# Token mixing of the second batch by one joint product, and its last two attention pairs as whole pairs

## Chip, cores, metric

The program runs on one core of one Trainium2 chip. The metric is device time in microseconds (us) of one execution, and the median over runs is compared. Engines are named as the profile names them: PE is TensorE (PEld its weight loads), DVE is VectorE, ACT is ScalarE, POOL is GpSimd, SP issues the DMAs.

## What is computed

Three stages follow each other for 4 batches of 768 tokens. Gated linear attention has 8 heads of 48 channels, so 384 channels together; a token and channel MLP follows, and a gating unit behind it.

```python
state = alpha[:, :, t, :, None] * state + np.einsum('bhd,bhe->bhde', k[:, :, t], v[:, :, t])
y[:, :, t] = np.einsum('bhd,bhde->bhe', q[:, :, t], state)
...
h = xt @ U @ V
u = x + h.transpose(0, 2, 1)
ch = np.maximum(u @ w_ch1, 0.0) @ w_ch2
return (u + ch).astype(np.float32)
```

The product with U (768 x 32) over the tokens, and with V (32 x 768) back to them, is the token mixing; the two products with w_ch1 and w_ch2 are the channel MLP. The gating unit is not touched by the change.

## The kernel before

Data lie with channels on the 128 partitions, in KE = 3 blocks of channels (m = 0, 1, 2) and NB = 2 blocks of 384 tokens. Products that need float32 accuracy are made of two fp32r parts, a high part and the remainder, in three matmuls (mm3, L287 to L289, and up_group, L380), or as plain float32 matmuls, which the trace shows as more than one pass of PE.

**Order of the work.** Every engine runs its instructions in the order in which the Python code issues them. The first batch's attention runs alone (first_batch). Then the channel MLP of batch b is issued group by group, and between its matmuls pull() is called, which advances a generator by a step: attend(b + 1), the attention and token mixing of the next batch. For b = 0 the pulls also move the loading and splitting of the MLP's weights, by the table FIRST_STEPS (L75): "f" is finish, one piece of a late step (ACT's high part L785, then DVE's remainder L252), "b" begins the next weight (DVE L237, L240, L247), "s" is a step of the attention. due() spaces the steps: with b = 0 some 40 steps go into 65 pulls, with later b 42 into 129, so the attention of the second batch is issued about twice as densely as that of the third and fourth.

**One attention pair.** attend handles a batch as NP = 4 pairs of heads, n = b * NP + i, in the order (3, 0, 1, 2) of their channel blocks. Eight steps make a pair: flip (L958 transposes k, ACT copies it, L961); prepare for the next pair (DVE's scan L914, reciprocal L917, and a multiplication L903 of k, on DVE or POOL); added (L1002, sums of k and v per chunk) and state, in which ACT writes the decay into a PSUM bank (L1009) and copies the sums (L1010), and DVE runs six scans (L1013); keep, two ACT copies of the state (L1023, L1024); scores (L974) and mask (DVE); the second part of prepare (scan L927, L903 of q); outputs; loading of a later pair.

A Pair has outputs in two parts: inner (L1034, masked scores and v) and outer (L1044, state and q). A WholePair has the scores of one head beside the q of the other in one operand, and v beside the state in the other, so one product per chunk (L1103) makes both. For that its place() copies half of q by a DMA (sq, L1080) and loads v into the free half of the state's tile (two DMAs, L1083), and its mask takes four operations (L1091) in place of two (L984). In the kernel before, the pairs of the third and fourth batch are WholePairs, since place() is called for n + 1 >= 2 * NP.

**Token mixing.** In the second batch, class Mix takes each channel block by itself, one pair later: flip (L1213, three transpositions per token block), a copy by ACT (L1220), product (L1229, six float32 matmuls of 128 columns with U) and keep (L1236, DVE L1237). In later batches JointMix collects all three blocks: ACT copies the high part of a flipped block (L1258), DVE makes the remainder in two operations (L1260), and one product over 384 columns (L1266 and L1279, fp32r) and keep (L1282, L1284) follow behind the last pair. split_u makes U's parts for that (ACT L1289 and three of L1292, DVE L1293). mix_sum (L318) then multiplies with V, DVE adds (L322), ACT makes the high part (L323) and POOL the remainder (L252). At the batch's end the MLP's results are added by L440; L387 and L368 are its high part and remainder of h.

**Banks.** PSUM banks 5 and 6 are the pair's (PAIR), 7 is ALONE. Flips use ALONE and the first of PAIR; the second mixing flip and the product of Mix use ALONE, and so does the decay:

```python
decay = ps.banks[:, ALONE, TB : TB + DS * NCH]
...
mix.take(mix.flip(1, ALONE))
pair.state(pair.added())
```

Of the kernel before, what the change touches and what calls it, by code (L numbers as in the profile page):

```python
# [46 lines left out]
E = H * D  # L47
# [29 lines left out]
    60: "b", 70: "ff", 80: "b", 89: "ff", 92: "b", 101: "fbf", 110: "ff",  # L77
# [23 lines left out]
def gla_mixer_gating_kernel(ctx: ExitStack, tc: tile.TileContext, akq, v, v2, vT, u, v3, w12, w_in, wsT, b_sp, w_out, out):  # L101
# [699 lines left out]
    with ExitStack() as fast:  # L801
# [95 lines left out]
        def scale(x, by, n):  # L897

            cut = NCH if n == 0 or by is bw and NP <= n < 2 * NP - 1 else 0
            half = NCH // 2 if n == 0 and by is fw else 0  # L900
            for engine, c in ((nc.vector, slice(0, half)), (nc.vector, slice(half, cut)), (nc.gpsimd, slice(cut, NCH))):
                if c.stop > c.start:
                    engine.tensor_tensor(out=chunks(x)[:, c], in0=chunks(x)[:, c], in1=chunks(by)[:, c, 1:CW], op=ALU.mult)  # L903
# [398 lines left out]
        def attend(b, blocks):  # L1302
# [3 lines left out]
            joint = b > 1  # L1306
            stk = up.pool.tile([(3 + joint) * R, E], F32R, name="stk", tag="stk")
            moves, mix = [], None
            if joint:
                if "u4" not in g:  # L1310
                    split_u()
                whole = JointMix(us, stk)
# [8 lines left out]
            for i in range(NP):  # L1321
# [5 lines left out]
                pair.flip()  # L1327
                if mix:
# [20 lines left out]
                if mix and not joint:  # L1349
                    gp = mix.product(0, ALONE)  # L1350
                pair.outputs()
                if mix and not joint:
                    mix.keep(gp)
                yield
                if n + 1 < NPAIR and n + 1 >= 2 * NP:
# [6 lines left out]
                mix = (whole if joint else Mix(us, pair.hp, stk)) if pair.hp < KE else None  # L1362
                if joint:
                    whole.m = pair.hp
                yield
            mix.take(mix.flip(0))
            mix.take(mix.flip(1))
            yield
            if joint:
                yield  # L1370
            gp = mix.product()
            if joint:
                yield
            mix.keep(gp)
            yield
            yield from mix_sum_steps(g, us, stk, up, ps, "x", blocks, whole.parts if joint else None)

        N_STEPS = NP * 8 + 2 + 2 * KE
# [31 lines left out]
        def first_batch(blocks):  # L1410
# [93 lines left out]
            weights.add()  # L1504
            summed(0, 0)
            summed(1, 0)
            gp = mixes[2].product()
            mixes[2].keep(gp)
            for blk in range(NB):
                summed(blk, 1)  # L1510
                summed(blk, 2)
# [87 lines left out]
        for b in range(B):  # L1599
            if b == 0:  # L1600
                n_steps = N_STEPS + N_AHEAD
            elif b + 1 < B:
                nxt = []
                steps, n_steps = attend(b + 1, nxt), N_STEPS + (2 if b > 0 else 0)
# [7 lines left out]
            groups = int(NB * NF1 * 2 * KE * (0.95 if b == 0 else 0.9))  # L1612
# [195 lines left out]
```

## Time and profile before

| what | us |
|---|---|
| median of 3 runs | 675.04 (674.24 to 675.76) |
| the profiled execution's own time | 675.9 |
| its span in the profile | 674.2 |
| PE busy (matmul) | 659.4, 98% of the span |
| DVE busy | 421.3, 62% |
| ACT busy | 306.4, 45% |
| POOL busy | 147.3, 22% |

The span runs from the first to the last instruction of the profiled execution; 1.7 us of its time lie around it. PE's share is so high that its few gaps are of interest, and what stands in them: the engine that releases it. The shares of the other engines are means over stages. While the first batch's MLP and the second batch's attention run together, from about 46 to 154 us, DVE also splits the MLP's weights and is much busier than its mean.

### The profile page before, as it was taken

To read this page: it belongs to the slowest core of one execution; us is meant where nothing else is said; L and a number is where in the kernel's file an instruction comes from. 1 tells how busy PE (TensorE), PEld (TensorE's weight loads), DVE (VectorE), ACT (ScalarE), POOL (GpSimd) and SP (SyncE) were. 2 spreads that over 40 slices of the span, in tenths; PEclk is the share of its full clock that TensorE was granted. 3 is DMA by queue.
4 is the path that set the end of the run, shared out by engine and by line. 5 is a ranking of instruction groups with operands and counts; after the bars stand their busy time and mean duration, and the time that the engine had idled before them with its cause. 6 is when DMAs were issued, how large, how long until landed. Compare 5 with 4: busy or idle time off the path is not lost.

```text
span 674.2 us, 13930 instructions
## 1 busy us (share of the span) xinstructions
PE 659.4 (98%) x5732; PEld 628.3 (93%) x5732; DVE 421.3 (62%) x808; ACT 306.4 (45%) x599; POOL 147.3 (22%) x139
## 2 busy tenths in 40 slices
PE   8989999899999999999999999999999999999996
PEld 7889999799999999999999999999999989999996
DVE  7989999668556435565236787486384356537541
ACT  3985467555555335555323445343343233334321
POOL 4530112133112132210120000306401620540051
PEclk9999999899999999999999999999999999999999
DMA  8799016433555501512112455401010202101011
GB/s 328 261 358 237 22 35 113 88 72 102 118 102 119 119 1 42 115 29 67 36 65 79 124 167 164 129 1 36 35 57 15 71 0 71 36 35 36 1 36 41
DMA packets 23561, 60.06 MB, mean 89 GB/s; under 512 B 3137, under 2 KB 13249, under 8 KB 22209
## 3 DMA queue, kind: packets, MB, share of 16 engines
q1 hardware_dynamic: 23488, 59.08, 32.0%
q8 instruction: 47, 0.77, 0.5%
q14 instruction: 26, 0.20, 0.1%
HBM read 46.88 MB, written 9.44 MB: 84 GB/s over the span
## 4 chain that ended last, share of the span: by engine, by line
PE 83%; DVE 12%; ACT 2%; issue 1%; DMA 0%; DVEq 0%; ACTq 0%
PE banks L380 19%; PE banks L287 18%; PE banks L289 18%; PE banks L288 18%; DVE bw L914 2%; PE banks L1103 2%; DVE fw L927 2%; DVE narrow L240 1%; PE banks L1002 1%; PE banks L974 1%; DVE w L252 1%; DVE narrow L247 1%; PE banks L958 1%; DVE hl L368 1%; PE banks L1229 1%
## 5 line engine op out<-in xcount | busy, mean ns | idle before, releaser
L380 PE MATMUL banks<-partuh,w 128*128 128x384 f32 x564 | 130.5, 339 | 1.9 <-DVE hl L368 1.8
L380 PEld LDWEIGHTS banks<-partuh,w 128*128 128x128 f32 x564 | 99.3, 188 | 3.6 <-DVE hl L368 2.4
L287 PE MATMUL banks<-h,w 128*128 128x384 f32 x288 | 98.1, 340 | 0.2
L289 PE MATMUL banks<-hl,w 128*128 128x384 f32 x288 | 96.4, 335 | 0.0
L288 PE MATMUL banks<-h,w 128*128 128x384 f32 x288 | 96.4, 335 | 0.0
L368 DVE SCALAR_TENSOR_TENSOR hl<-banks,h 128x384 fp32r<-128x384 f32 x96 | 52.7, 550 | 58.0 <-ACT h L387 56.9
L387 ACT ACTIVATE h<-banks 128x384 fp32r<-128x384 f32 x94 | 45.8, 487 | 78.6 <-PE banks L380 78.4
L252 POOL TENSOR_TENSOR partul<-ub,partuh 128x384 fp32r<-128x384 f32 x43 | 43.0, 1024 | 137.1 <-ACT partuh L457 83.7
L252 POOL TENSOR_TENSOR room<-room 128x384 fp32r<-128x384 f32 x32 | 32.6, 1018 | 164.4 <-ACT room L600 164.2
L380 PE MATMUL banks<-partul,w 128*128 128x384 f32 x282 | 66.0, 341 | 0.0
L903 POOL TENSOR_TENSOR akq<-akq,fw 128x768 f32<-128x768 f32 x14 | 23.7, 1693 | 148.2 <-DVE fw L927 96.8
L287 PEld LDWEIGHTS banks<-h,w 128*128 128x128 f32 x288 | 54.1, 188 | 1.6 <-issue 0.8
L288 PEld LDWEIGHTS banks<-h,w 128*128 128x128 f32 x288 | 54.1, 188 | 0.0
L289 PEld LDWEIGHTS banks<-hl,w 128*128 128x128 f32 x288 | 54.1, 188 | 0.0
L380 PEld LDWEIGHTS banks<-partul,w 128*128 128x128 f32 x282 | 49.2, 188 | 0.8
L600 ACT ACTIVATE room<-room 128x384 fp32r<-128x384 f32 x32 | 16.8, 526 | 67.5 <-DVE room L598 67.5
L252 DVE TENSOR_TENSOR vl<-vt,vh 128x512 fp32r<-128x512 f32 (+1 forms) x48 | 26.6, 616 | 20.7 <-ACT vh L505 20.7
L288 PE MATMUL banks<-partuh,winl 128*128 128x384 f32 x96 | 32.4, 338 | 0.0
L289 PE MATMUL banks<-partul,winh 128*128 128x384 f32 x96 | 32.4, 338 | 0.0
L287 PE MATMUL banks<-partuh,winh 128*128 128x384 f32 x96 | 32.4, 338 | 0.0
L288 PE MATMUL banks<-wouth,room 128*128 128x384 f32 x96 | 32.3, 336 | 0.0
L289 PE MATMUL banks<-woutl,room 128*128 128x384 f32 x96 | 32.3, 336 | 0.0
(256 smaller groups left out, 1479.2 us busy)
## 6 DMA issues: line engine op xcount, KB each, us to landing
akq<-in_akq SPq DMA_DIRECT2D x24, 434.4 KB, 7.7
bits<-in_w SPq DMA_DIRECT2D x12, 768.0 KB, 11.5
x2d<-ub SPq DMA_DIRECT2D x8, 576.0 KB, 3.7
ub<-x2d SPq DMA_DIRECT2D x8, 576.0 KB, 4.2
out_y<-room SPq DMA_DIRECT2D x24, 192.0 KB, 1.9
v<-in_v SPq DMA_DIRECT2D x15, 288.0 KB, 8.1
words<-in_wsT SPq DMA_DIRECT2D x7, 576.0 KB, 3.7
words<-in_w_in SPq DMA_DIRECT2D x8, 384.0 KB, 3.2
```

The lines of the kernel that those rows point to most:

```text
L252: engine.tensor_tensor(out=out, in0=x, in1=hi.bitcast(F32), op=ALU.subtract)
L287: nc.tensor.matmul(out=ps, lhsT=wh, rhs=xh, start=first, stop=False, skip_group_check=more)
L288: nc.tensor.matmul(out=ps, lhsT=wl, rhs=xh, start=False, stop=False, skip_group_check=more)
L289: nc.tensor.matmul(out=ps, lhsT=wh, rhs=xl, start=False, stop=last, skip_group_check=more)
L368: nc.vector.scalar_tensor_tensor(out=hl, in0=ps[:, 0:TB], scalar=0.0, in1=h.bitcast(F32), op0=ALU.max, op1=ALU.subtract)
L380: nc.tensor.matmul(out=ps[:, 0:TB], lhsT=wx[:, k * 128 : (k + 1) * 128], rhs=ux[:, k, :], start=i == 0, stop=i == len(parts) - 1)
L387: nc.scalar.activation(out=h, in_=ps[:, 0:TB], func=AF.Relu)
L600: nc.scalar.activation(out=hi, in_=x, func=AF.Copy)
L903: engine.tensor_tensor(out=chunks(x)[:, c], in0=chunks(x)[:, c], in1=chunks(by)[:, c, 1:CW], op=ALU.mult)
L914: nc.vector.tensor_tensor_scan(out=bw[:, ::-1], data0=a[:, 1 : AW + 1][:, ::-1], data1=ends[:, ::-1], initial=0.0, op0=ALU.mult, op1=ALU.max)
L927: nc.vector.tensor_tensor_scan(out=fw, data0=a[:, 0:AW], data1=starts, initial=0.0, op0=ALU.mult, op1=ALU.max)
L1103: nc.tensor.matmul(out=self.py[HW * h : HW * h + D, x, j * CH : (j + 1) * CH], lhsT=vw[:, h, c, :], rhs=self.sms[h][:, t], start=True, sto ...
```

## The change

1. The second batch (b = 1) uses JointMix for all three channel blocks. Its first two blocks are flipped in the fourth pair's steps (block 0 in place of the earlier flips, block 1's first half ahead of the fourth pair's outputs, the rest behind it), and one joint product follows. split_u runs at the fourth pair's flip.
2. The second batch's third and fourth pairs are WholePairs (n + 1 >= NP + 2), so their place() adds three DMAs each.
3. The third pair's q is multiplied by DVE in place of POOL (L903).
4. FIRST_STEPS: of "fbf" at pull 101 the last "f" goes to pull 107. The steps of the second batch rise by two, the pulls that they are spread over from 136 to 139.
5. In the first batch, all three products come ahead of the six sums, and these go in another order; the add of a weight (POOL) goes behind the third product.

```diff
-    60: "b", 70: "ff", 80: "b", 89: "ff", 92: "b", 101: "fbf", 110: "ff",
+    60: "b", 70: "ff", 80: "b", 89: "ff", 92: "b", 101: "fb", 107: "f", 110: "ff",
...
-            cut = NCH if n == 0 or by is bw and NP <= n < 2 * NP - 1 else 0
+            cut = NCH if n == 0 or by is bw and NP <= n < 2 * NP - 1 or by is fw and n == NP + 2 else 0
...
-            joint = b > 1
-            stk = up.pool.tile([(3 + joint) * R, E], F32R, name="stk", tag="stk")
+            late = b == 1
+            stk = up.pool.tile([4 * R, E], F32R, name="stk", tag="stk")
             moves, mix = [], None
-            if joint:
-                if "u4" not in g:
-                    split_u()
-                whole = JointMix(us, stk)
+            whole = JointMix(us, stk)
...
                 pair.flip()
+                if late and i == NP - 1:
+                    split_u()
                 if mix:
                     mix.take(mix.flip(0, PAIR[1]))
...
-                if mix and not joint:
-                    gp = mix.product(0, ALONE)
+                if late and mix:
+                    whole.m += 1
+                    mix.take(mix.flip(0, ALONE))
                 pair.outputs()
-                if mix and not joint:
-                    mix.keep(gp)
                 yield
-                if n + 1 < NPAIR and n + 1 >= 2 * NP:
+                if n + 1 < NPAIR and n + 1 >= NP + 2:
                     placed[n + 1] = WholePair(n + 1, None, None, tags)
...
-                mix = (whole if joint else Mix(us, pair.hp, stk)) if pair.hp < KE else None
-                if joint:
-                    whole.m = pair.hp
+                if late:
+                    mix, whole.m = whole if i == NP - 2 else None, 0
+                else:
+                    mix, whole.m = whole if pair.hp < KE else None, pair.hp
                 yield
+            if late:
+                mix, whole.m = whole, KE - 2
+                mix.take(mix.flip(1))
+                whole.m = KE - 1
             mix.take(mix.flip(0))
             mix.take(mix.flip(1))
...
-            weights.add()
-            summed(0, 0)
-            summed(1, 0)
             gp = mixes[2].product()
             mixes[2].keep(gp)
-            for blk in range(NB):
-                summed(blk, 1)
-                summed(blk, 2)
+            weights.add()
+            for blk, m in ((0, 0), (0, 1), (1, 0), (0, 2), (1, 1), (1, 2)):
+                summed(blk, m)
...
-            groups = int(NB * NF1 * 2 * KE * (0.95 if b == 0 else 0.9))
+            groups = int(NB * NF1 * 2 * KE * (0.97 if b == 0 else 0.9))
```

The order on DVE ahead of the second batch's third pair's scans, before (w is an MLP weight, narrow its raw form, sm the masked scores):

```order
L927 SCALAR_TENSOR_TENSOR fw<-akq_89,starts 128x780
L368 SCALAR_TENSOR_TENSOR hl<-banks,h 128x384
L914 SCALAR_TENSOR_TENSOR bw<-akq_87,ends 128x780
L917 RECIPROCAL starts<-bw 128x12
L368 SCALAR_TENSOR_TENSOR hl<-banks,h 128x384
L440 TENSOR_TENSOR ub<-banks,ub 128x384 x3
L237 TENSOR_SCALAR narrow<-bits 128x768
L240 SCALAR_TENSOR_TENSOR narrow<-bits,narrow 128x768
L247 ISA narrow<-bits,narrow 128x1536
L252 TENSOR_TENSOR w_1455<-narrow,w_1455 128x768
L1013 SCALAR_TENSOR_TENSOR after<-add,banks 128x96 x6
L984 TENSOR_TENSOR sm<-banks,causal 128x384 x2
```

and in the changed kernel, from the multiplication that comes in behind that first scan (sq is the copied half of q):

```order
L903 TENSOR_TENSOR akq_89<-akq_89,fw 128x768
L368 SCALAR_TENSOR_TENSOR hl<-banks,h 128x384
L914 SCALAR_TENSOR_TENSOR bw<-akq_87,ends 128x780
L917 RECIPROCAL starts<-bw 128x12
L368 SCALAR_TENSOR_TENSOR hl<-banks,h 128x384
L440 TENSOR_TENSOR ub<-banks,ub 128x384 x3
L237 TENSOR_SCALAR narrow<-bits 128x768
L240 SCALAR_TENSOR_TENSOR narrow<-bits,narrow 128x768
L247 ISA narrow<-bits,narrow 128x1536
L1013 SCALAR_TENSOR_TENSOR after<-add,banks 128x96 x6
L1091 TENSOR_TENSOR akq_89<-banks,causal 64x6x64 x2
L1091 TENSOR_TENSOR sq<-banks,causal 64x6x64 x2
```

The multiplication L903 of q is new, the remainder L252 ahead of the scans is gone, and four masks of L1091 stand where two of L984 did.

The order on DVE at the fourth pair, before (stk is the product with U):

```order
L927 SCALAR_TENSOR_TENSOR fw<-akq_87,starts 128x780
L1237 TENSOR_TENSOR stk<-banks,stk 32x128
L252 TENSOR_TENSOR w_1632<-narrow,w_1632 128x768
L368 SCALAR_TENSOR_TENSOR hl<-banks,h 128x384
L440 TENSOR_TENSOR ub<-banks,ub 128x384 x3
L914 SCALAR_TENSOR_TENSOR bw<-akq_88,ends 128x780
L917 RECIPROCAL starts<-bw 128x12
L1013 SCALAR_TENSOR_TENSOR after<-add,banks 128x96 x6
L984 TENSOR_TENSOR sm<-banks,causal 128x384 x2
```

and in the changed kernel (u is the split U, ynl and yl are remainders of a flipped block, of token block 0 with partuh and of block 1 with partul):

```order
L252 TENSOR_TENSOR w_1603<-narrow,w_1603 128x768
L1293 TENSOR_TENSOR u_1617<-uf,u_1617 128x6x32
L1260 TENSOR_TENSOR ynl<-banks,partuh 128x2x128
L1260 TENSOR_TENSOR yl<-banks,partuh 128x128
L368 SCALAR_TENSOR_TENSOR hl<-banks,h 128x384
L440 TENSOR_TENSOR ub<-banks,ub 128x384 x3
L914 SCALAR_TENSOR_TENSOR bw<-akq_88,ends 128x780
L917 RECIPROCAL starts<-bw 128x12
L1260 TENSOR_TENSOR ynl<-banks,partul 128x2x128
L1260 TENSOR_TENSOR yl<-banks,partul 128x128
L1013 SCALAR_TENSOR_TENSOR after<-add,banks 128x96 x6
```

The split of U and two groups of L1260 stand ahead of the scans, the second group behind the next pair's scan L914.

The order on PE at the third pair's outputs, before:

```order
L974 MATMUL banks<-akq_89 64x64 x24
L287 MATMUL banks<-h,w_1025 128x384
L288 MATMUL banks<-h,w_1025 128x384
L289 MATMUL banks<-hl,w_1025 128x384
L1229 MATMUL banks<-yb,u_100 96x128 x6
L1034 MATMUL banks<-sm,v 48x64 x24
L1044 MATMUL banks<-akq_89,state 48x64 x22
L287 MATMUL banks<-h,w_1025 128x384
```

and in the changed kernel, where the last two rows go on in turn, 24 in all:

```order
L974 MATMUL banks<-akq_89 64x64 x24
L287 MATMUL banks<-h,w_1027 128x384
L288 MATMUL banks<-h,w_1027 128x384
L289 MATMUL banks<-hl,w_1027 128x384
L1103 MATMUL banks<-akq_89,state 48x64
L1103 MATMUL banks<-sq,state 48x64
```

The product L1229 and the two parts of the outputs are replaced by the whole pair's products.

## Rows read from the trace of the kernel before

**Rows 1.** Timeline of PE: start, us, engine, line, op, out<-in, count [idle<-releaser].

```profile
121.73 2.43 PE L1229 MATMUL banks<-yb,u 128*96 128x128 f32 x12 [1.84 <-DVE after L1013]
...
126.97 0.44 PE L287 MATMUL banks<-h,w 128*128 128x384 f32 x1
...
135.41 0.93 PE L974 MATMUL banks<-akq 64*64 64x64 f32 x48
...
137.94 1.47 PE L1229 MATMUL banks<-yb,u 128*96 128x128 f32 x12
...
139.34 0.89 PE L1034 MATMUL banks<-sm,v 64*48 64x64 f32 x48
...
141.54 0.79 PE L380 MATMUL banks<-partul,w 128*128 128x384 f32 x3
```

**Rows 2.** Windows: length, busy PE, PEld, DVE, ACT, POOL; PEclk, DMA share, GB/s.

```profile
121.70:126.00 4.30, 4.27 (x74) 3.85 (x76) 1.43 (x4) 3.78 (x6) 0.00 (x0) 0.60 0.01 4
```

**Rows 3.** Timeline of DVE ahead of the third pair's scans.

```profile
111.70 3.10 DVE L914 TENSOR_TENSOR_SCAN bw<-akq,ends 128x780 f32<-128x780 f32 x1
...
120.11 1.57 DVE L1013 TENSOR_TENSOR_SCAN after<-add,banks 128x96 f32<-128x96 f32 x6
```

**Rows 4.** Timeline of PE: first and last output product, first and last joint product, third batch.

```profile
166.86 0.26 PE L1103 MATMUL banks<-akq,state 128*48 128x64 f32 x1
...
167.98 0.22 PE L1103 MATMUL banks<-akq,state 128*48 128x64 f32 x1
...
229.63 0.34 PE L1266 MATMUL banks<-partuh,u 128*128 128x384 f32 x1
...
231.55 0.34 PE L1266 MATMUL banks<-partul,u 128*128 128x384 f32 x1
```

**Rows 5.** Timeline of PE: a group of three transpositions.

```profile
113.30 0.49 PE L1213 MATMUL banks<-ident,ub 128*128 128x128 f32 x3
```

**Rows 6.** Timeline of POOL in that stretch.

```profile
111.47 1.70 POOL L903 TENSOR_TENSOR akq<-akq,fw 128x768 f32<-128x768 f32 x1 [10.80 <-DVE fw L927]
```

**Rows 7.** Timeline of DVE at the fourth pair.

```profile
130.61 0.96 DVE L252 TENSOR_TENSOR w<-narrow,w 128x768 fp32r<-128x768 f32 x1 [0.93 <-ACT w L785]
...
132.07 1.48 DVE L440 TENSOR_TENSOR ub<-banks,ub 128x384 f32<-128x384 f32 x3
...
133.47 1.77 DVE L914 TENSOR_TENSOR_SCAN bw<-akq,ends 128x780 f32<-128x780 f32 x1
```

**Rows 8.** By source line: ns min/median/max, first and last start; last line: L1080.

```profile
L903 DVE TENSOR_TENSOR akq<-akq,bw x4: 896/898/924, 6.1 to 102.6; 128x768 f32<-128x768 f32 x4
...
L1091 DVE TENSOR_TENSOR akq<-banks,causal x16: 552/558/566, 163.7 to 317.1; 64x384 f32<-64x384 f32 x16
...
L1260 DVE TENSOR_TENSOR ynl<-banks,partul x6: 415/424/426, 194.3 to 325.9; 128x256 fp32r<-128x256 f32 x6
...
L1260 DVE TENSOR_TENSOR yl<-banks,partul x6: 281/281/281, 194.7 to 326.2; 128x128 fp32r<-128x128 f32 x6
...
L1292 ACT ACTIVATE u<-uf x3: 347/348/364, 154.7 to 155.2; 128x192 fp32r<-128x192 f32 x3
...
L1258 ACT ACTIVATE partul<-banks x6: 485/491/492, 193.8 to 325.2; 128x384 fp32r<-128x384 f32 x6
...
DMA to landing us min/median/max: 2.6/2.7/2.8
```

**Rows 9.** Timeline of ACT: second copy of the third pair's state.

```profile
122.88 1.11 ACT L1024 ACTIVATE state<-after 64x528 f32<-64x528 f32 x1
```

**Rows 10.** Timeline of ACT: fourth pair, and the decay's copy in the third batch.

```profile
130.47 0.86 ACT L961 ACTIVATE kn<-banks 128x384 f32<-128x384 f32 x2
...
133.78 0.70 ACT L1010 ACTIVATE add<-banks 128x576 f32<-128x576 f32 x1
...
195.05 0.26 ACT L1009 ACTIVATE banks<-seen 128x96 f32<-128x96 f32 x1 [0.75 <-DVE yl L1260]
```

**Rows 11.** Timeline of PE: first batch, ahead of the third block's sums.

```profile
45.23 0.79 PE L318 MATMUL banks<-vs,stk 96*128 96x384 f32 x3 [1.12 <-DVE stk L1237]
```

More of the change, by code (lines that the diff above doesn't have):

```diff
@@ L1368, in attend @@
             yield
-            if joint:
-                yield
+            yield
             gp = mix.product()
-            if joint:
-                yield
+            yield
             mix.keep(gp)
             yield
-            yield from mix_sum_steps(g, us, stk, up, ps, "x", blocks, whole.parts if joint else None)
-        N_STEPS = NP * 8 + 2 + 2 * KE
+            yield from mix_sum_steps(g, us, stk, up, ps, "x", blocks, whole.parts)
+        N_STEPS = NP * 8 + 4 + 2 * KE
         def check_alpha():
@@ L1603, in gla_mixer_gating_kernel @@
                 nxt = []
-                steps, n_steps = attend(b + 1, nxt), N_STEPS + (2 if b > 0 else 0)
+                steps, n_steps = attend(b + 1, nxt), N_STEPS
             else:
```

## Prediction

> **What bounds the kernel now.** I read the page's engine shares and the chain of waits first: TensorE (PE) is busy nearly the whole span, so a change pays by what it takes off PE or by what it makes PE wait. Then I looked for the places where PE does wait while the second batch's attention is pulled into the first batch's channel MLP, because the diff works there. There is one. At the outputs of the third pair PE stands 1.84 us, released by VectorE (DVE) at the six scans of line L1013 [rows 1]: the product of L1229 takes the bank in which the scans read their decay. TensorE then runs at a granted clock of 0.60 on average for the next 4.30 us [rows 2], between its two levels of 1.2 and 2.4 GHz, and loses 4.30 x (1 - 0.60) = 1.7 us. So this place costs 1.84 + 1.7 = 3.5 us. In DVE's timeline the reader is to see that neither the scans nor the scan of L914 ahead of them have an idle time in brackets [rows 3]: DVE is the late engine, and what lies in its queue there is on the path. At the fourth pair PE does not wait: scores at 135.41, product at 137.94, inner at 139.34, next MLP group at 141.54 [rows 1].
>
> **The change, part by part.** *PE work.* The profile shows one product to take 139.34 - 137.94 = 1.40 us, inner plus outer 141.54 - 139.34 = 2.20 us [rows 1]. Three products and two inner-outer pairs go: 4.2 + 4.4 = 8.6. Two outputs of the whole-pair kind come, 167.98 - 166.86 + 0.05 = 1.2 us each in the third batch, and one joint product, 231.55 - 229.63 + 0.18 = 2.1 us [rows 4]. Added 4.5, so the net is -4.1 us if nothing waits. The 18 transpositions stay, but six leave the third pair's steps for later ones; a group of three is 0.49 us [rows 5] and overlaps its neighbours, so PE gets to the third pair's outputs some 0.7 us earlier.
>
> *Third pair.* Its outputs now begin with a product over scores and state at once, so they need all four masks of L1091 and both copies L1023 and L1024; before, a product and the inner sums lay ahead of the part that needs the copies. When is that? The scans started at 120.11. On DVE three things change ahead of them. The scan of L914 at 111.70 took 3.10 us while GpSimd (POOL) multiplied from 111.47 to 113.17 [rows 3, 6]; the same scan takes 1.77 elsewhere [rows 7]. That multiplication moves to DVE: -1.33, +0.90 [rows 8]. One L252 leaves for a later step: -0.96 [rows 7]. Scans at 118.7, done after 1.6 at 120.3. The copies ended at 122.88 + 1.11 = 123.99, 2.3 after the scans' end [rows 3, 9]; now 122.6. Four masks at 0.56 [rows 8] and a little between them end at 122.5 to 122.8. PE can start at 122.7, and is there at 121.73 - 1.84 - 0.7 = 119.2: 3.5 us idle. A wait of 1.84 was followed by the low clock, so I charge the same 1.7 again. Together 5.2 against 3.5: **+1.7**; up to 2.0 if the low clock lasts a little longer, 1.3 if shorter.
>
> That POOL blocks the scan is what the Trainium skill states in "SBUF — State Buffer", section "SBUF: two separate sides": GpSimd and a DVE operation with two SBUF inputs share a port pair, held for a whole instruction. The row agrees: 3.10 less 1.77 is 1.33, and 1.47 us of the scan lie inside POOL's operation. Should the long scan have another cause, the move would give nothing back and cost 0.90: scans at 120.0, and the whole sum 1.3 us higher.
>
> *Fourth pair.* The outputs of the third end at 122.7 + 1.2 + 1.1 (half clock) = 125.0. From there to the fourth pair's scores PE does what it did from 126.97 to 135.41, 8.44 us [rows 1], and half a us of low clock: it is there at 134.0. But the scores write banks that L1010 on ScalarE (ACT) must have read, L1010 stands behind L1009, and L1009 writes the bank of the second flipped block. In the third batch it was seen to wait 0.75 us for DVE's L1260 there [rows 10]. So the scores wait for this chain. ACT: from the outputs' end to the end of the copies L961 it took 131.33 - 126.97 = 4.4 [rows 1, 10], an MLP group of PE inside it, so with the low clock 5.3: 130.3. Then the new split of U, four operations of 0.35 [rows 8], now in the middle of this pair: 131.6; two copies of the flipped blocks at 0.49 less overlap [rows 8]: 132.4. DVE: the first block's two L1260 (0.42 + 0.28 [rows 8]) by 132.6, then, in program order, L368 at 0.5, three L440 at 1.4, the next pair's scan L914 at 1.77 and its reciprocal at 0.2 [rows 7], and only then the second block's L1260, 0.65: 137.1. ACT's L1009 and L1010 [rows 10]: 0.9. Scores at 138.1, **4.1 us idle**. In the cheapest case ACT holds DVE up nowhere: L927, two L252, the split, two L1260 pairs, L368, L440 and L914 from 124.5 on make 134.5, 0.5 us idle. I take 4.1, since every operation between has its row and none can pass another on its engine.
>
> Then scans (1.6) and masks (2.4) put the fourth outputs at 142.2. PE's own work from scores to there is 137.94 - 135.41 = 2.5 and 0.35 of transpositions, so it idles another 1.2, or, where the clock falls after the 4.1 us, spends up to 2.5 on it. I take 1.7: **+5.8** for this pair, 0.5 to 6.6.
>
> *Behind it.* The joint product is read by ACT and DVE before the sums L318 can start, with two MLP pieces between. The nearest row is L318 waiting 1.12 us for the same DVE step in the first batch [rows 11]. Bounds 0 and 1.1; **+0.6**. The two steps more are taken up by the pulls (139 in place of 136).
>
> *First batch.* All three products go ahead of the six sums, so the wait of 1.12 us [rows 11] may go. But the first MLP group behind it needs the copies of all six sums and the remainders, which DVE makes one after another, in the same number. I take nothing; -1.1 to +0.5, the latter if POOL's delayed add runs into DVE's remainders.
>
> *DMA.* Each of the two pairs puts three transfers on SP's queue, ahead of a later load. The third's wait for the scaled q, ready on DVE about 112, and land about 2.7 us after issue [rows 8], by 117: 5 us before use. The fourth's wait for POOL's product at about 128 and land by 133. Nothing.
>
> Sum: -4.1 + 1.7 + 5.8 + 0.6 = **+4.0**. The profiled run took 675.9, 0.9 above the median of 675.04; +4.0 on the median gives **679.0 us**.
>
> **The rivals.** *PE's saving decides* (faster). If the fourth pair's chain comes in time, only 0.5 of the 5.8 is paid, and nothing behind it: -4.1 + 1.7 + 0.5 = -1.9, 673.1 us; with the first batch's wait gone 672.0. For it: before, this pair did not wait at all, and most of DVE's operations were there already. Against it: two L1260 pairs, the split of U and the order, the second block behind L914, are new, and whole outputs have no product ahead of them as cover. It decides when the fourth pair's waits and the tail together stay under 2.4 us.
>
> *A draw.* ACT holds DVE up half as much as I reckon, scores wait 2 us, the clock does not fall a second time, 0.5 before the outputs: -4.1 + 1.7 + 2.5 + 0.3 = +0.4, 675.4 us.
>
> *Everything late* (slower still). Port not the cause, second low clock at full price, tail and first batch at their upper ends: -4.1 + 2.0 + 1.3 + 6.6 + 1.1 + 0.5 = +7.4, 682.4 us; belongs to the forecast's side.
>
> That the change doesn't do what it says I can set aside: the order of instructions shows the products gone and the joint one in place.
>
> **How the numbers follow.** A measurement of this kernel can tell some 0.2%, 1.35 us, from no change. Forecast (slower, including everything late) 0.57, PE's saving 0.27, draw 0.16. Given the forecast, 677 to 682. The range takes in the first rival with both its values and reaches up near the sum of all upper bounds: 672.0 to 682.0. Faster 0.27, same 0.16, slower 0.57.
>
> **What would show it.** Right: PE waits over 3 us ahead of the third pair's L1103, released by DVE's L1091 or ACT's L1024, with the low clock after; ahead of the fourth pair's scores L974 a second wait of 2 to 5 us on ACT's L1010, which itself waits through L1009 for DVE's L1260; the scan of L914 for the fourth pair is back at 1.77. Wrong: no wait at L974, or the fourth outputs end before 140; then the saving of 4.1 comes through. Also wrong if the first batch's MLP starts more than 1 us earlier.

## The result and the profile after

The changed kernel took **682.73 us** (median of 4 runs, 681.61 to 683.25) beside 675.4 us (674.24 to 676.52) for the kernel before: ratio 1.0116, interval 1.0101 to 1.0130, so 7.8 us slower by the ratio and 7.3 by the medians. The forecast was slower, 679.0, range 672 to 682: the side is right, the size is not. The profiled execution is the fastest of the four, 681.61 against 675.9 of the one shown before, with a span of 679.8 against 674.2. So the traces have 5.6 us to explain, the three other executions of the change lie another 0.7 to 1.6 above, and the kernel before's profiled execution lies 0.5 above its median.

In PE's timeline of the changed kernel (columns as in [rows 1]; I leave out what has no idle time in brackets, but for the first MLP group behind the outputs of the third and of the fourth pair) the whole loss stands in one list:

```profile
121.99 0.31 PE L1103 MATMUL banks<-akq,state 128*48 128x64 f32 x2 [2.33 <-DVE akq L1091]
122.57 0.45 PE L1103 MATMUL banks<-sq,state 128*48 128x64 f32 x2 [0.27 <-DVE sq L1091]
123.26 0.31 PE L1103 MATMUL banks<-akq,state 128*48 128x64 f32 x1 [0.24 <-DVE sq L1091]
...
125.78 0.51 PE L287 MATMUL banks<-h,w 128*128 128x384 f32 x1
...
132.55 0.80 PE L1002 MATMUL banks<-v,kn 64*64 64x48 f32 x40 [0.67 <-DVE yl L1260]
...
137.78 0.93 PE L974 MATMUL banks<-akq 64*64 64x64 f32 x48 [2.57 <-POOL akq L903]
...
141.86 0.26 PE L1103 MATMUL banks<-akq,state 128*48 128x64 f32 x1 [0.85 <-issue]
...
143.48 0.79 PE L380 MATMUL banks<-partul,w 128*128 128x384 f32 x3
...
145.62 1.21 PE L1213 MATMUL banks<-ident,ub 128*128 128x128 f32 x9 [0.30 <-ACT ub L1059]
...
153.08 0.62 PE L318 MATMUL banks<-vs,stk 128*128 128x384 f32 x2 [0.50 <-DVE stk L1284]
...
160.14 0.84 PE L958 MATMUL banks<-ident,akq 128*128 128x128 f32 x6 [1.57 <-issue]
```

Read it against [rows 1]. The third pair's outputs end at 125.78, 1.19 us earlier than before (126.97). The fourth pair's scores start at 137.78, 2.37 later (135.41), its outputs end at 143.48, 1.94 later (141.54). The next batch's first flips L958 come at 160.14; before they came at 154.60, so the delay has grown to 5.54, and the span's 5.6 is complete there. The tail before, with its one wait:

```profile
145.33 1.55 PE L1229 MATMUL banks<-yb,u 128*96 128x128 f32 x12 [0.25 <-ACT yb L1220]
...
154.60 0.82 PE L958 MATMUL banks<-ident,akq 128*128 128x128 f32 x6
```

So the profile's loss has two places: the fourth pair (from -1.19 to +2.37) and the tail behind it (from +1.94 to +5.54).

The granted clock is the other thing to see. In the windows of the changed kernel (columns as in [rows 2]) it falls behind the third pair's wait exactly as before, 0.60 over the same 4.30 us, and nowhere else in this stretch:

```profile
121.70:126.00 4.30, 3.50 (x49) 3.03 (x50) 2.90 (x5) 2.89 (x7) 0.00 (x0) 0.60 0.15 45
126.00:137.70 11.70, 8.54 (x93) 7.83 (x93) 7.76 (x15) 6.57 (x16) 3.85 (x2) 1.00 0.64 122
137.70:144.00 6.30, 5.37 (x111) 4.91 (x112) 4.73 (x12) 4.58 (x8) 0.05 (x1) 1.00 0.25 45
144.00:160.00 16.00, 13.76 (x80) 12.72 (x78) 11.29 (x26) 6.91 (x16) 5.64 (x5) 1.00 0.52 105
```

What holds the fourth pair's scores is read from three engines. DVE's timeline has the first flipped block's L1260 at 131.78, then the MLP's L368 and L440, the next batch's scan L914 without a gap, and the second block's L1260 only at 136.13:

```profile
131.78 0.42 DVE L1260 TENSOR_TENSOR ynl<-banks,partuh 128x256 fp32r<-128x256 f32 x1 [0.52 <-ACT partuh L1258]
...
132.32 0.55 DVE L368 SCALAR_TENSOR_TENSOR hl<-banks,h 128x384 fp32r<-128x384 f32 x1
132.78 1.48 DVE L440 TENSOR_TENSOR ub<-banks,ub 128x384 f32<-128x384 f32 x3
134.18 1.77 DVE L914 TENSOR_TENSOR_SCAN bw<-akq,ends 128x780 f32<-128x780 f32 x1
...
136.13 0.36 DVE L1260 TENSOR_TENSOR ynl<-banks,partul 128x256 fp32r<-128x256 f32 x1
136.41 0.28 DVE L1260 TENSOR_TENSOR yl<-banks,partul 128x128 fp32r<-128x128 f32 x1
```

ACT's timeline shows L1009 idle 4.63 us for that, and L1010 ending at 137.64, 0.14 ahead of the scores:

```profile
136.78 0.26 ACT L1009 ACTIVATE banks<-seen 128x96 f32<-128x96 f32 x1 [4.63 <-DVE yl L1260]
136.97 0.67 ACT L1010 ACTIVATE add<-banks 128x576 f32<-128x576 f32 x1
```

The view of PE names POOL's L903 as releaser instead, since that operation ended a little later, at 136.08 + 1.67 = 137.75:

```profile
136.08 1.67 POOL L903 TENSOR_TENSOR akq<-akq,bw 128x768 f32<-128x768 f32 x1 [6.99 <-DVE bw L914]
```

But it scales k of the next batch's first pair, which the fourth pair's scores do not read. Which of the two it is, the first experiment decides.

In the tail, the flips L958 wait 1.57 us for "issue". DVE's timeline shows what they could wait for: the adds L322 of the last two sums stand behind L368 and three L440 and end at 160.03, 0.11 before the flips.

```profile
157.16 0.55 DVE L368 SCALAR_TENSOR_TENSOR hl<-banks,h 128x384 fp32r<-128x384 f32 x1
157.63 1.48 DVE L440 TENSOR_TENSOR ub<-banks,ub 128x384 f32<-128x384 f32 x3
159.02 1.01 DVE L322 TENSOR_TENSOR ub<-banks,ub 128x384 f32<-128x384 f32 x2
```

### The profile page after: what moved, and what is told of

It reads as the page before. It is cut to its first block, busy times and chain, and to the rows that moved or that the text cites. A ratio compares the mean times of both kernels' runs of the same rounds, so it can differ in the third digit from the quotient of the medians.

```text
span 679.8 us, 13737 instructions
## 1 busy us (share of the span) xinstructions
PE 658.3 (97%) x5620; PEld 625.4 (92%) x5620; DVE 427.9 (63%) x823; ACT 305.4 (45%) x597; POOL 147.5 (22%) x138
## 4 chain that ended last, share of the span: by engine, by line
PE 78%; DMA 7%; DVE 6%; issue 3%; ACT 3%; SPq 1%; POOL 1%; POOLq 0%; DVEq 0%; ACTq 0%
PE banks L380 18%; PE banks L287 18%; PE banks L288 18%; PE banks L289 18%; DMA akq<-in_akq 6%; PE banks L1103 2%; DMA bits<-in_w 1%; PE banks L1002 1%; PE banks L974 1%; PE banks L958 1%; DVE after L1013 1%; DVE bw L914 1%; DVE hl L368 1%; SPq L164 1%; PE banks L1213 1%
## 5 line engine op out<-in xcount | busy, mean ns | idle before, releaser
L380 PE MATMUL banks<-partuh,w 128*128 128x384 f32 x564 | 130.5, 339 | 1.4 <-DVE hl L368 1.3
L380 PEld LDWEIGHTS banks<-partuh,w 128*128 128x128 f32 x564 | 99.3, 188 | 3.1 <-DVE hl L368 1.8
L287 PE MATMUL banks<-h,w 128*128 128x384 f32 x288 | 98.1, 341 | 0.2
L368 DVE SCALAR_TENSOR_TENSOR hl<-banks,h 128x384 fp32r<-128x384 f32 x96 | 52.8, 551 | 53.9 <-ACT h L387 53.5
L252 POOL TENSOR_TENSOR partul<-ub,partuh 128x384 fp32r<-128x384 f32 x43 | 44.5, 1059 | 141.5 <-ACT partuh L457 84.0
L252 POOL TENSOR_TENSOR room<-room 128x384 fp32r<-128x384 f32 x32 | 32.5, 1017 | 163.6 <-ACT room L600 163.3
L380 PE MATMUL banks<-partul,w 128*128 128x384 f32 x282 | 66.1, 342 | 0.0
L287 PEld LDWEIGHTS banks<-h,w 128*128 128x128 f32 x288 | 54.1, 188 | 1.6 <-issue 0.8
L903 POOL TENSOR_TENSOR akq<-akq,fw 128x768 f32<-128x768 f32 x13 | 22.5, 1731 | 136.4 <-DVE fw L927 88.0
L380 PEld LDWEIGHTS banks<-partul,w 128*128 128x128 f32 x282 | 49.1, 188 | 0.8
L252 DVE TENSOR_TENSOR vl<-vt,vh 128x512 fp32r<-128x512 f32 (+1 forms) x48 | 26.6, 618 | 20.7 <-ACT vh L505 20.7
L903 POOL TENSOR_TENSOR akq<-akq,bw 128x768 f32<-128x768 f32 x11 | 18.6, 1689 | 65.8 <-DVE bw L914 58.4
L287 PE MATMUL banks<-partuh,winh 128*128 128x384 f32 x96 | 32.4, 338 | 0.0
```

The lines of the kernel that those rows point to most:

```text
L252: engine.tensor_tensor(out=out, in0=x, in1=hi.bitcast(F32), op=ALU.subtract)
L287: nc.tensor.matmul(out=ps, lhsT=wh, rhs=xh, start=first, stop=False, skip_group_check=more)
L368: nc.vector.scalar_tensor_tensor(out=hl, in0=ps[:, 0:TB], scalar=0.0, in1=h.bitcast(F32), op0=ALU.max, op1=ALU.subtract)
L380: nc.tensor.matmul(out=ps[:, 0:TB], lhsT=wx[:, k * 128 : (k + 1) * 128], rhs=ux[:, k, :], start=i == 0, stop=i == len(parts) - 1)
```

## The experiments

Theory A: the loss is waits that the joint mixing makes, in the fourth pair (second L1260 behind the scan L914) and in the tail (last sums behind the MLP's L440). Rival B: the whole outputs themselves cost. Further rivals stand with each run. Diffs are against the change where nothing else is said; there is no experiment 14, and 15 repeats 11. The runs were taken in four groups (1 to 4, 5 to 8, 9 to 12, 13 and 15), each beside the kernel before, whose median there was 675.74, 674.62, 675.87 and 676.01 us. So a difference across groups, as from the change's 682.73, is good to about 1 us; what is finer is read from the traces.

**1. Scan of the next batch behind the masks**

```diff
-                next(ahead, None)
+                if not (late and i == NP - 1):
+                    next(ahead, None)
...
                 pair.mask(pair.scores())
                 move_some(moves, 3)
+                if late and i == NP - 1:
+                    next(ahead, None)
```

> The change, with one thing moved: in the fourth pair of the second batch the backward scan for the next batch's first pair (L914 and its reciprocal) stands behind the masks L1091 in place of ahead of the second flipped block's L1260. Theory A, the joint mixing's L1260 is late behind that scan: L1260 for the second block starts at about 134.2 in place of 136.1, ScalarE's L1010 ends at 135.8, the scores L974 start near 135.9 with a wait of under 1 us in place of 2.57, and the fourth outputs end 1.5 to 2 us earlier (143.48 to about 141.7); the time falls by 1.5 to 2.5 against the change's 682.7. Rival C, the scores wait for the releaser that the profile names, GpSimd's L903 of the next batch's first pair: that operation now starts after 141, so the scores start later than 137.8, and the time rises by 3 or more.

Measured: 681.08 us, 1.65 below the change. PE's timeline:

```profile
136.14 0.93 PE L974 MATMUL banks<-akq 64*64 64x64 f32 x48 [0.67 <-ACT add L1010]
...
141.54 0.81 PE L380 MATMUL banks<-partul,w 128*128 128x384 f32 x3
...
144.39 0.87 PE L1213 MATMUL banks<-ident,ub 128*128 128x128 f32 x6 [0.99 <-ACT ub L1059]
145.86 0.55 PE L1213 MATMUL banks<-ident,ub 128*128 128x128 f32 x3 [0.60 <-DVE yl L1260]
...
159.71 0.52 PE L958 MATMUL banks<-ident,akq 128*128 128x128 f32 x3 [1.57 <-issue]
```

The wait falls from 2.57 to 0.67 and is now put down to L1010, while the named POOL operation runs at 141.97, long behind the scores. Rival C is out. The fourth outputs end at 141.54, 1.94 earlier than in the change, but L958 only 0.43 earlier: the tail takes 1.5 us back, in two waits of 0.99 and 0.60 ahead of L1213. Part of that is of the move's own making: the scan L927 now meets POOL's multiplication and takes 2.68 us in DVE's timeline, which pushes the tail's L1260 back:

```profile
142.61 2.68 DVE L927 TENSOR_TENSOR_SCAN fw<-akq,starts 128x780 f32<-128x780 f32 x1
```

**2. Whole outputs, but three products as before**

```diff
-            stk = up.pool.tile([4 * R, E], F32R, name="stk", tag="stk")
+            joint = b > 1
+            stk = up.pool.tile([(3 + joint) * R, E], F32R, name="stk", tag="stk")
...
-                if late and i == NP - 1:
-                    split_u()
...
+                if mix and not joint:
+                    gp = mix.product(0, ALONE)
                 pair.outputs()
+                if mix and not joint:
+                    mix.keep(gp)
```

The batch's tail, N_STEPS and the pace (0.95) are as in the kernel before too.

> The change without the joint product in the second batch: third and fourth pair with whole outputs L1103, the three products L1229 and their copies as before, pulls and steps as before; the first batch's new order of sums and the scaling on VectorE stay. Theory A, what costs is the joint mixing's queue in the fourth pair and its tail, while the whole outputs pay: third outputs end at 125.0 to 125.8, the scores of the fourth pair start without a wait near 134, its outputs end near 140.2, the next batch's first flips L958 come at 153.2 to 153.6, and the time is 1 to 1.5 below the kernel before (about 674). Rival B, the whole outputs themselves cost because they need all masks and both copies: 676 to 679, with waits of over 2.5 us ahead of L1103 in both pairs.

Measured: 673.19 us, ratio 0.9970 to the kernel before (0.9959 to 0.9981): 2 us **faster**. The waits left in the third pair, and the fourth's scores without any:

```profile
120.31 1.55 PE L1229 MATMUL banks<-yb,u 128*96 128x128 f32 x12 [1.04 <-DVE after L1013]
...
122.83 0.23 PE L1103 MATMUL banks<-akq,state 128*48 128x64 f32 x1 [0.37 <-DVE sq L1091]
...
133.22 0.93 PE L974 MATMUL banks<-akq 64*64 64x64 f32 x48
```

Third outputs at 124.19, scores at 133.22, L958 at 151.85: all earlier than theory A asked for, since no low clock followed in this execution. Rival B is out as the cause of the change's loss. What the whole outputs are worth by themselves is not shown here: this kernel also has L252 moved and q multiplied on DVE, by which the scans L1013 start at 118.69 in place of 120.11, and the low clock is gone. Experiments 13 and 15 come back to that. The product, started at 120.31, is over when the masks come: it costs PE nothing there.

**3. Joint product, but pairs as before**

```diff
-            cut = NCH if n == 0 or by is bw and NP <= n < 2 * NP - 1 or by is fw and n == NP + 2 else 0
+            cut = NCH if n == 0 or by is bw and NP <= n < 2 * NP - 1 else 0
...
-                if n + 1 < NPAIR and n + 1 >= NP + 2:
+                if n + 1 < NPAIR and n + 1 >= 2 * NP:
```

> The change with the third and fourth pair of the second batch computed by L1034 and L1044 as before (no placing, the scaling back on GpSimd), the joint product kept. Theory A: third outputs end at 124.5 to 125.5, the scores of the fourth pair still wait 1.5 to 3 us for ScalarE behind L1260, the tail's waits (0.3 + 0.5 + 1.6) stay, and the time is 678 to 681. Rival B, the whole outputs are what costs: within 1 us of the kernel before, 674.5 to 676.5.

Measured: 682.51 us, above A's 681 and as slow as the change. L974 waits the same 2.57 us, L958 the same 1.57. What A's number left out shows in the windows: here the third pair kept the full clock, and it fell behind the fourth pair's wait instead:

```profile
121.00:126.00 5.00, 3.97 (x98) 3.52 (x99) 2.14 (x5) 4.78 (x9) 0.00 (x0) 1.00 0.05 14
...
136.00:142.00 6.00, 5.19 (x106) 4.73 (x108) 2.49 (x8) 4.31 (x8) 0.78 (x1) 0.72 0.01 3
```

**4. First batch's order alone**, in the kernel before:

```diff
-            weights.add()
-            summed(0, 0)
-            summed(1, 0)
             gp = mixes[2].product()
             mixes[2].keep(gp)
-            for blk in range(NB):
-                summed(blk, 1)
-                summed(blk, 2)
+            weights.add()
+            for blk, m in ((0, 0), (0, 1), (1, 0), (0, 2), (1, 1), (1, 2)):
+                summed(blk, m)
```

> The kernel before with the first batch's new order alone (third product ahead of the six sums, the add behind it). From the change's trace, where the first MLP group starts 0.26 us earlier: 0.1 to 0.4 below the kernel before, not to be told from no change. Rival: the full 1.1 us of the old wait of L318 comes back, 674.3.

Measured: 675.59 against 675.74, ratio 1.0002 (0.9992 to 1.0012): no change, as forecast.

**5. Sums two steps earlier**

```diff
-    60: "b", 70: "ff", 80: "b", 89: "ff", 92: "b", 101: "fb", 107: "f", 110: "ff",
+    60: "b", 70: "ff", 80: "b", 89: "ff", 92: "b", 101: "fb", 107: "f", 110: "ff", 132: "s", 134: "s",
```

> The change with two steps more drawn at pulls 132 and 134, so that all six sums L318 and their adds L322 stand ahead of the last L368 and the three L440 of the first batch's MLP on VectorE. Theory A, part one, the tail: the wait of 1.57 us ahead of the next batch's first flips L958, which ends 0.1 us after the last two L322, falls below 0.3; the waits of 0.30 and 0.50 ahead of it stay; the time falls by 1.2 to 1.7 (to about 681.2). Rival D, the flips wait for something else (code, a transfer, GpSimd's product): the wait stays over 1 us and the time stays within 0.5 of 682.7.

Measured: 680.65 us, 2.1 below the change, more than the 1.2 to 1.7 that were expected. L958 starts without a wait, so the tail's 1.57 us were the adds behind L440; rival D is out:

```profile
158.98 0.81 PE L958 MATMUL banks<-ident,akq 128*128 128x128 f32 x6
```

The windows of this run have the low clock twice, behind the third pair and behind the 2.55 us ahead of the fourth's scores:

```profile
121.80:130.00 8.20, 7.25 (x73) 6.80 (x73) 4.52 (x7) 6.05 (x13) 2.24 (x1) 0.79 0.13 28
130.00:138.00 8.00, 5.03 (x71) 4.36 (x69) 6.13 (x12) 3.34 (x10) 1.46 (x1) 0.99 0.95 182
138.00:142.00 4.00, 3.75 (x57) 3.67 (x58) 3.51 (x10) 2.33 (x3) 0.21 (x1) 0.59 0.25 54
```

The second costs 4.00 x (1 - 0.59) = 1.6 us.

**6. Experiments 1 and 5 together** (both diffs)

> Both moves at once, the scan of the next batch behind the fourth pair's masks and the sums two steps earlier. Theory A: with the tail cleared the gain of the fourth pair gets through, the scores wait about 0.7, L958 under 0.4, and the time is 678.5 to 680, 2.7 to 4.2 below the change, still 3 or more above the kernel before. Rival E, the tail is bound by VectorE's and ScalarE's own chain and what one place gives another takes: 680.5 to 681.5.

Measured: 679.43 us, as theory A says, 3.3 below the change. E's range is missed. Its waits ahead of L1213 (1.02 and 0.59) and L318 (0.51) stay, as E would have it; they are the smaller part.

**7. Third pair's q scaled by POOL again**

```diff
-            cut = NCH if n == 0 or by is bw and NP <= n < 2 * NP - 1 or by is fw and n == NP + 2 else 0
+            cut = NCH if n == 0 or by is bw and NP <= n < 2 * NP - 1 else 0
```

> The change with the third pair's q scaled by GpSimd as in the kernel before. If GpSimd's product blocks the scan: L914 behind it takes about 3.1 in place of 1.77, the third pair's scans L1013 start at 119.4 to 119.6 (0.4 later than the change), PE's wait ahead of L1103 grows by the same, the time by 0 to 0.5. If the long scan had another cause: L914 at 1.77, the scans start near 118.2, the wait shrinks by 0.9, the time by 0.5 to 0.9.

Measured: 682.42 us, not to be told from the change's 682.73. DVE's timeline, though, is clear:

```profile
111.99 3.08 DVE L914 TENSOR_TENSOR_SCAN bw<-akq,ends 128x780 f32<-128x780 f32 x1
...
119.52 1.57 DVE L1013 TENSOR_TENSOR_SCAN after<-add,banks 128x96 f32<-128x96 f32 x6
```

In the change the same scan took 1.77 and L1013 started at 119.12; PE's first wait at L1103 grows from 2.33 to 2.65. POOL's product does block the scan, by 1.3 us, and the move was worth 0.4.

**8. Whole outputs in the fourth pair alone** (against experiment 2)

```diff
-                if n + 1 < NPAIR and n + 1 >= NP + 2:
+                if n + 1 < NPAIR and n + 1 >= NP + 3:
```

> As the second experiment (three products as before, no joint product in the second batch), but with whole outputs in the fourth pair alone; the third goes by L1034 and L1044. Theory A: behind VectorE's scans the third pair's two forms end within 0.5 us of each other (product hidden, inner sums ready with two masks, copies about when the product is done), so the time is 673 to 673.8 and the whole outputs pay in the fourth pair only. Rival: each pair's whole outputs are worth its 1 us of TensorE work, 674.2.

Measured: 674.03 us, 0.23 above A's range, 0.2 below the rival. The first part held: the third outputs end at 124.08 here and at 124.19 in experiment 2, and L958 comes at 151.96 and 151.85. The two times, 0.84 apart and from different groups, would speak for the rival; but in the traces that difference is a wait of 0.83 us ahead of L380 at 418.34 in this execution, long behind the pairs, where the two kernels are the same. One trace of each is at hand, so how much of the medians' difference that is stays open.

**12, 10, 11, 9. The weight preparation behind the masks.** In all four the pull table alone is changed further, on top of the change, of experiment 6, of the kernel before and of experiment 2. In the kernel before "fbf" becomes "f" and "bf"; in the other three:

```diff
-    60: "b", 70: "ff", 80: "b", 89: "ff", 92: "b", 101: "fb", 107: "f", 110: "ff",
+    60: "b", 70: "ff", 80: "b", 89: "ff", 92: "b", 101: "f", 105: "b", 107: "f", 110: "ff",
```

> The change, with the weight preparation of pull 101 (L237, L240, L247 on VectorE, 2.5 us in one piece) drawn at pull 105, behind the third pair's masks in place of ahead of its scans. If VectorE's queue ahead of the scans sets the third pair's wait: scans L1013 at about 116.7 in place of 119.1, the wait ahead of L1103 2.8 in all falls to about 1.3, the low clock behind it mostly goes, the third outputs end near 123 in place of 125.8; the waits at the fourth pair (2.6) and in the tail (1.6) stay; the time falls by 2 to 4 (679 to 680.5). Rival F, the weights are then late for the MLP: PE waits at L287 or L380 behind 125 and the time stays within 1 of 682.7.

Measured: 679.98 us, 2.75 below the change. The third pair's first wait is down from 2.33 to 0.60, and no low clock follows it; but the sums L1002 now wait 1.47 us in place of 0.67 for the first flipped block's L1260, and the low clock came behind L974 (0.72 over 136 to 142):

```profile
120.44 0.31 PE L1103 MATMUL banks<-akq,state 128*48 128x64 f32 x2 [0.60 <-DVE akq L1091]
...
130.57 0.80 PE L1002 MATMUL banks<-v,kn 64*64 64x48 f32 x40 [1.47 <-DVE yl L1260]
...
135.80 1.08 PE L974 MATMUL banks<-akq 64*64 64x64 f32 x48 [2.56 <-POOL akq L903]
```

> All three moves on top of the change: next batch's scan behind the fourth pair's masks, sums two steps earlier, weight preparation at pull 105. If the three waits are the whole loss, and the joint product itself saves TensorE work: 675.5 to 677.5, about the kernel before. Rival: the joint form keeps 2 us or more in waits of ScalarE's and VectorE's copies (L1213, L318): not below 678.

Measured: 677.8 us, just above the first theory's range, and just below the rival's 678. The three moves take 4.9 of the change's 7.3 us; 1.47 at L1002, 1.02 and 0.60 at L1213 and 0.50 at L318, 3.6 us of waits for the joint mixing's copies, are left.

> The kernel before with the weight preparation of pull 101 and the finish behind it drawn at pull 105: scans at about 116.7, the wait of 1.84 us ahead of L1229 falls below 0.3, no low clock behind it, 671.8 to 673.3 (1.5 to 3.5 below the kernel before). Rival F: 674.5 or more.

Measured: 672.19 us, ratio 0.9949 (0.9931 to 0.9967): **the fastest kernel here**, by a table entry alone. DVE starts the scans at 116.88 in place of 120.11, and PE's product has no wait at all:

```profile
119.79 1.47 PE L1229 MATMUL banks<-yb,u 128*96 128x128 f32 x12
```

> The second experiment (whole outputs in both pairs, three products as before) with the weight preparation at pull 105. The waits of 1.04 and 0.37 us in the third pair go, no low clock: 671.5 to 672.2, the fastest so far. Rival F, weights late: 673 or more.

Measured: 673.41 us: a miss, no gain on experiment 2. Not for rival F's reason: PE waits 1.78 us at the fourth pair's flips L958, for DVE's L1237, which empties the bank of the third pair's product. (L958 of the next batch still comes at 151.53, 0.32 earlier than in experiment 2; a wait of 0.38 ahead of L380 at 417.46 takes that back.) L252 stands ahead of L1237, so I moved that too.

**13 and 15. Is L252 it?** Experiment 2 with both at pull 105, and experiment 11 again on the same chip.

```diff
-    60: "b", 70: "ff", 80: "b", 89: "ff", 92: "b", 101: "fb", 107: "f", 110: "ff",
+    60: "b", 70: "ff", 80: "b", 89: "ff", 92: "b", 101: "f", 105: "bf", 110: "ff",
```

> The kernel of the second experiment with the weight preparation and the finish L252 behind it both at pull 105, so that L252 no longer stands between the scan L927 and the copy L1237 of the third pair's product on VectorE. If the whole outputs pay once VectorE's queue is out of the way: the wait of 1.78 us ahead of the fourth pair's flips L958 goes, 670.5 to 671.7, below the kernel before with the same move (672.2). Rival: the whole outputs are worth nothing by themselves, 672 to 672.6.

> The kernel before with the weight preparation at pull 105 once more, beside the thirteenth on the same chip: 672.0 to 672.6.

Measured: 674.10 us (ratio 0.9982, 0.9972 to 0.9991) and 672.17 (0.9954, 0.9940 to 0.9967). Both guesses about 13 were too low. In its trace the wait is still there (L252 now runs at 123.75, ahead of L927, and so still ahead of L1237):

```profile
127.42 0.85 PE L958 MATMUL banks<-ident,akq 128*128 128x128 f32 x6 [1.78 <-DVE stk L1237]
```

Lines of DVE's and PE's timelines of 13 and, under them, of 11 say why (where L287 starts, the third pair's outputs have ended):

```profile
118.86 1.22 DVE L1091 TENSOR_TENSOR akq<-banks,causal 64x384 f32<-64x384 f32 x2 [0.82 <-PE banks L974]
120.11 1.14 DVE L1091 TENSOR_TENSOR sq<-banks,causal 64x384 f32<-64x384 f32 x2
...
122.77 0.44 PE L287 MATMUL banks<-h,w 128*128 128x384 f32 x1
...
126.99 0.28 DVE L1237 TENSOR_TENSOR stk<-banks,stk 32x128 fp32r<-32x128 f32 x1
```

```profile
119.27 1.02 DVE L984 TENSOR_TENSOR sm<-banks,causal 128x384 f32<-128x384 f32 x2 [0.82 <-PE banks L974]
...
123.39 0.44 PE L287 MATMUL banks<-h,w 128*128 128x384 f32 x1
...
125.82 0.28 DVE L1237 TENSOR_TENSOR stk<-banks,stk 32x128 fp32r<-32x128 f32 x1
```

The whole pair's four masks take 1.22 + 1.14 = 2.36 us where L984 takes 1.02. Between masks and L1237 DVE is then without a gap, so L1237 comes 1.17 us later (126.99 against 125.82), while PE's outputs end 0.62 earlier (122.77 against 123.39): the two together are PE's wait of 1.78. What PE saves is small, since it waits for the masks: in 13 the outputs take 1.99 us from their first product at 120.78, in 11 inner plus outer take 2.20 from 121.19. Without such waits it would be more: in experiment 2 the 44 of 48 products behind the last mask run in 124.19 - 122.83 = 1.36. So a whole pair moves 1.3 us onto DVE to save less than 0.8 on PE, in a stretch where DVE is the late engine. Side by side in one group, the kernel with both whole pairs is 1.9 us slower than the one without (674.10 against 672.17). They also differ in q's engine and in the first batch's order, which experiments 7 and 4 found to cost nothing. So rival B, though not the cause of the change's loss, holds in the small.

## Why the prediction was right, and where it was wrong

**The fourth pair: mechanism right, its size in part by luck.** The forecast had 4.1 us idle ahead of the scores through L1260 behind L914, L1009 and L1010, scores at 138.1 and outputs ending some 1.2 behind 142.2. Measured: 0.67 + 2.57 = 3.24 us, scores at 137.78, outputs from 141.86 to 143.48. Experiment 1 shows that it is this chain. That the scores' time fits to 0.3 is luck, since two errors cancel: the third pair's outputs ended 0.8 later than forecast, and ACT then took 4.44 us to the end of the copies L961 (125.78 to 130.22) in place of 5.3. The further wait ahead of the outputs was forecast as 1.2 on PE's own time; the profile has 0.85, under "issue", ending 0.19 behind the last mask.

**The third pair: right in kind.** Start of its outputs forecast at 122.7, seen at 121.99; end at 125.0, seen at 125.78; low clock behind, seen. The sign to look for was a wait of over 3 us; 2.33 + 0.27 + 0.24 = 2.84 came, since PE arrives at 119.66 and not at 119.2, and its first products need only two of the four masks. That POOL blocks the scan held: 1.77 in the change, 3.08 with the product back on POOL. The Trainium skill states in "SBUF — State Buffer", section "SBUF: two separate sides", that GpSimd and a DVE operation with two SBUF inputs lock each other out of a shared port pair. Both figures agree with that, and so does the 2.68 of L927 in experiment 1, beside POOL's L903 from 141.97 to 143.66. Without that move the scans would start 0.4 later, below what a measurement of the time can tell.

**PE's work: the term counted what the wait had covered.** "-4.1 if nothing waits" was added to stalls reckoned against PE's arrival, and so paid back as idle time; that part is consistent. But it made the rival "PE's saving decides" look like a case: experiment 2 shows that the third pair's product lies wholly ahead of masks that are later, and in experiment 3, where it is taken out and the clock stays full, the outer sums L1044 run on from 123.47, in experiment 4, with it and at full clock, from 123.67: 0.2 us for 1.4 us of work.

**The tail: the step that failed.** "Behind it", +0.6 with bounds 0 and 1.1, looked only at the joint product's copies ahead of L318, and they came out as that, 0.50. The step "the two steps more are taken up by the pulls (139 in place of 136)" was wrong: with the pace at 139, the last two sums came in one piece at the very end of the MLP, their adds behind L368 and three L440 on DVE, and the next batch's flips needed their banks: 1.57 us. Whether the two steps more or the slower pace puts them there, no run separates. With 0.30 ahead of L1213 that is 2.37 in place of 0.6. Experiment 5 took the 1.57 away. From the fourth outputs to L958 the delay grows by 3.6; 2.1 of it are these waits (2.37 less 0.25 that stood ahead of L1229 before), about 0.8 the joint product in place of the last single one (2.1 against 1.3), 0.4 three more transpositions; 0.3 I have not assigned.

**The low clock: known, but not charged a second time.** The forecast took the cheaper case behind the fourth pair's wait. The profile bears it out, but the change's other three executions had mean granted clocks of 0.990 to 0.994 in place of 0.997, and were 0.7 to 1.6 us longer. Experiments 3, 5 and 12 show the low clock at 136 to 142 in their traces, worth some 1.6. In the change's own other executions it is not shown: no trace of them is at hand, and the means fit badly, since 0.990 in place of 0.997 is 4.8 us of missing clock over the span, some three such stretches, while the time rose by 1.6.

Together: the forecast's 4.0, and 1.8 more for the tail, make 5.8 against the traces' 5.6. From there to the 7.3 of the medians, 0.5 is the kernel before, whose profiled execution lies that much above its median, and 1.1 the change, whose profiled execution lies that much below; a second low clock would explain the latter, and that stays an argument. Another 0.4 of the miss is that the forecast stood on a median of 675.04 where this comparison's is 675.4. The rival "everything late", 682.4, gave the size with other terms (port, first batch) than those that came, so it was right by luck.

**First batch at nothing: right** (experiment 4).

## What to carry to other kernels

Look for the late engine of a stretch before saving on the busy one: here PE was 98% busy, yet where the change worked DVE set the time, and moving 3.4 us of DVE's weight preparation (L237, L240, L247 and a L252) behind the masks gained 3.7 us by the medians (1.84 of wait, and the low clock behind it), more than any form of the changed mixing or outputs. Work taken off an engine that then waits for the same thing is not saved. Where a counter paces steps, ask what is left for the end and what stands in the queues between the last step and the next user of its buffers.

## What the runs showed of the hardware that I had not expected

The low clock does not follow each wait of the same length. Before, the 1.84 us ahead of L1229 were followed by 0.60 over 4.30 us [rows 2]; in experiment 4 the same line waited 1.89, and the window behind it reads full clock:

```profile
121.40:126.00 4.60, 4.60 (x109) 4.30 (x110) 1.72 (x4) 4.54 (x8) 0.00 (x0) 1.00 0.02 4
```

In experiments 3, 5 and 12 it followed the fourth pair's wait of 2.6 us, in the profiles of the change and of experiment 7 it did not. A kernel with such waits scatters: beside the experiments the kernel before ran from 674.13 to 675.36 where its mean granted clock was 0.997 or more, and from 675.51 to 676.65 where it was 0.995 or 0.996, so its median moves with the share of either kind. The kernel of experiments 11 and 15, without the third pair's wait, ran from 671.99 to 672.77.
